# Joint maxima over two PSUM banks, one exponential for a global row, and K and Q transposed head by head, in a fused block-sparse attention and MLP kernel

## The chip, the cores and the metric

The kernel runs on one core of a Trainium2 chip. The time is the device time of one execution in microseconds (us), lower is better. The engines are named as in the profile: PE is TensorE (PEld its weight loads), DVE is VectorE, ACT is ScalarE, POOL is GpSimd, SP is SyncE, which here only issues DMAs. PSUM, into which TensorE writes, has eight banks of 512 float32 per partition; the kernel gives them out one by one.

## The reference, cut to what matters

Attention over 4 batches, 8 heads, 768 positions, head size 64, in blocks of 32 positions (24 blocks), with a mask: a query block sees its neighbours, the first and the last block, and three sampled blocks; the first and the last query block see everything. Its output, heads side by side, goes through a gated MLP (called MoE in the code) of 512 to 2048 to 512.

```python
scores = scale * np.matmul(q, k.transpose(0, 1, 3, 2))
scores = np.where(mask, scores, -1000000000.0)
scores = scores - np.max(scores, axis=-1, keepdims=True)
attn = np.exp(scores)
attn = attn / (np.sum(attn, axis=-1, keepdims=True) + 1e-09)
x = np.matmul(attn, v)            # then (B, H, S, D) -> (B * S, H * D)
h = x @ w_in
g = h * (1.0 / (1.0 + np.exp(-beta * h)))
out = g @ w_out
```

## The kernel before, in words

**Work and stages.** Each batch is prepared once: K, Q and V are loaded, K and Q are transposed by TensorE (`tr`, L460 to L468, four tasks for each of K and Q, one for two heads) and evicted into KT and QT (`ev`, L470). V is also written to a table in DRAM (VT, L490, L494). Then come 11 pairs of ordinary query blocks, 44 in all. For pair n: K blocks are gathered in SBUF on POOL and DVE (`kg`, `kn`), V blocks by DMAs from VT on SP's queue (`vg`, L582), `sc` (L595) makes the scores of all eight heads in two banks, `mx` (L621) the row maxima of each bank on DVE, `ex` (L627) the exponentials on ACT, two for each bank, `rc` and `nrm` (L635, L638) the normalisation, `tp` (L647) the transposes, `ptv` (L657) their eviction, `av` (L661) the product with V, and `xv` (L678) the copies into xT, the MLP's input. The two global query blocks of a batch go another way: `gs` (L700) fills four banks at once, with all 768 keys in two halves of 384 for each half of the heads, then `gm` (L717), `ge` (L724), `gr` (L732), `gn`, `gt`, `gptv`, and `gav` (L753), which multiplies with V for all four sets, and `gx` (L767), which copies into xT. In `gav` the 128 output rows are two heads and the 128 columns hold both row sets for both heads, of which a head needs half.

**The MLP** runs over eight groups of 8 or 16 blocks (L795). For a group, `h` (L814, product with w_in), `tanh` and `stt` (L823, L828) go sixteen times over slices of 128 hidden columns; then `y` (L842, product with w_out), `oe` and `od` (L854, L861).

**Loads of K, Q and V.** Batch 0 comes through SP in float32 and is cast by DVE into K16 and Q16 (L395), eight casts. Later batches come as float16 through POOL's queue (L442), two halves each, into two raw buffers: RAW[1] for K, RAW[0] for V and then for Q, so that a load of Q waits for V's copy out of that buffer. DVE then permutes them (`perm`, L447) from head-major into K16, Q16 or Vn, whose columns are all heads side by side, so that a transpose takes two heads at once: 128 columns by 128 rows, six of them to a task.

**Order.** Nothing is scheduled by the framework. Every piece of work is a `Task` with engine, modelled duration, dependences and priority; `Plan.run` simulates the machine and gives out engines and banks, always to the ready task of lowest priority number. Each engine then runs its tasks strictly in that order. A task that `opens` banks waits in the plan until as many are free (L104 to L107), any of the eight, and takes those that have been free longest (L119 to L121); the MLP may hold four while attention is left. Tasks that may run on one of several engines (`ev`, `kn`, `nrm`, `xv`, `gx`, `gn`) are given to the one that the model finds earliest. The waits at run time follow the data, not the plan, so where the model is off, an engine stands at a task whose input is late, and all behind it stand too.

Of the kernel before, what the change touches and what calls it, by code (L numbers as in the profile page):

```python
# [22 lines left out]
class Task:  # L23
    def __init__(self, name, eng, dur, emit, deps=(), prio=0.0, lat=0.0,
                 opens=(), closes=(), moe=False, dma=0.0, slack=0.0, hw=0, bulk=None):
        self.on = {eng: dur} if isinstance(eng, str) else dict(eng)
        self.name, self.eng, self.dur, self.emit = name, None, None, emit
        self.deps = [d for d in deps if d is not None]
        self.prio, self.lat = prio, lat
        self.opens, self.closes, self.moe, self.dma = opens, closes, moe, dma  # L30
        self.slack, self.hw, self.bulk = slack, hw, bulk
        self.kind = name.rstrip("0123456789.")
        self.end = None


class Plan:
# [9 lines left out]
    def add(self, *a, **k):  # L46
        t = Task(*a, **k)
        self.tasks.append(t)
        return t

    def run(self):
# [36 lines left out]
        while done < len(tasks):  # L88
            progress = False
            for e in engines:  # L90
# [3 lines left out]
                for t in waiting[e]:  # L94
                    if ready_at[t] > now + 1e-9:
                        continue
                    if len(t.on) > 1:
                        cost = {o: max(free[o], now) + d + BIAS.get((t.kind, o), 0.0)
                                for o, d in t.on.items()}
                        if cost[e] > min(cost.values()) + 1e-9:  # L100
                            continue
                    if t.bulk is not None and ring_at > now + t.bulk + 1e-9:
                        continue
                    if t.opens:  # L104
                        n_ok = sum(1 for f, _ in bank_free if f <= now + 1e-9)
                        if n_ok < len(t.opens):
                            continue  # L107
                        if t.moe and attention_left and held_moe + len(t.opens) > self.moe_banks:
                            continue
                    if best is None or t.prio < best.prio:  # L110
                        best = t
# [6 lines left out]
                if t.opens:  # L118
                    bank_free.sort()  # L119
                    for name in t.opens:  # L120
                        _, i = bank_free.pop(0)  # L121
                        self.bank[name] = i
                        if t.moe:
                            held_moe += 1
                            moe_owner.add(name)
                    if not t.moe:
                        attention_left -= 1
# [55 lines left out]
def kernel(  # L183
# [47 lines left out]
    K16 = sb("K16", [P, J, D_MODEL])  # L231
    Q16 = sb("Q16", [P, J, D_MODEL])
    RAW = [sb(f"RAW{i}", [P, H, J * D]) for i in range(2)]
# [14 lines left out]
    banks = [psum.tile([P, 512], FP32, name=f"bank{i}") for i in range(8)]  # L248
# [4 lines left out]
    bank16 = lambda name: banks[plan.bank[name]][:, :].bitcast(FP16)  # L253

# [131 lines left out]
    for i, (nm, t, dst) in enumerate((("K", k, K16), ("Q", q, Q16), ("V", v, None))):  # L386
        for f in range(2):
# [6 lines left out]
            for hp in range(2 * f, 2 * f + 2):  # L394
# [3 lines left out]
                        out=dst[:, :, hp * P:(hp + 1) * P].rearrange("p j (h d) -> p h j d", h=2),  # L398
                        in_=stage32(i, hp).rearrange("p h (j d) -> p h j d", j=J)),
# [31 lines left out]
    trK, trQ, evK, evQ, vperm, vtab, perm = {}, {}, {}, {}, {}, {}, {}  # L431
    later = {b: [] for b in range(B)}
    for b in range(B):
        pr = prep_prio(b)
        if b:
            vperm[b] = []
            for nm, t, raw, dst in (("V", v, RAW[0], Vn[b % 2]), ("K", k, RAW[1], K16), ("Q", q, RAW[0], Q16)):
                tr = {"K": trK, "Q": trQ}.get(nm)
                for f in range(2):
                    hs = slice(f * HH, (f + 1) * HH)  # L440
                    free = [vperm[b][f]] if nm == "Q" else [perm["QK"["VK".index(nm)], b - 1, f]] if b > 1 else []
# [5 lines left out]
                    tpm = add(f"perm{nm}{b}.{f}", "DVE", 0.55, lambda raw=raw, dst=dst, hs=hs: copy_on(  # L447
                        "DVE", dst[:, :, hs.start * D:hs.stop * D].rearrange("p j (h d) -> p h j d", h=HH),
                        raw[:, hs, :].rearrange("p h (j d) -> p h j d", j=J)),
                        deps=[tl] + ([tr[b - 1, hp] for hp in range(2 * f, 2 * f + 2)] if tr else []),  # L450
                        prio=pr - 5 * (nm == "V"))
                    if nm == "V":
                        vperm[b].append(tpm)
                    else:
                        perm[nm, b, f] = tpm
                        for hp in range(2 * f, 2 * f + 2):
                            ld[nm, b, hp] = tpm
        for nm, s16, dstT, tr, ev in (("K", K16, KT, trK, evK), ("Q", Q16, QT, trQ, evQ)):
            for hp in range(NHP):
                def emit_tr(nm=nm, s16=s16, b=b, hp=hp):  # L460
                    o = bank16((nm, b, hp))
                    for j in range(J):
                        nc.tensor.transpose(  # L463
                            out=o[:, j * P:(j + 1) * P],
                            in_=s16[:, j, hp * P:(hp + 1) * P],
                            identity=identity)
# [36 lines left out]
    for n, (b, p) in enumerate(order_pairs):  # L503
# [91 lines left out]
        def emit_sc(n=n, b=b, p=p, i0=i0, kgb=kgb):  # L595
# [11 lines left out]
            for g in range(2):  # L607
                for hp in range(NHP):
# [9 lines left out]
                    opens=(("S", n, 0), ("S", n, 1)))  # L618

        for u in range(2):  # L620
            mx[n, u] = add(f"mx{n}.{u}", "DVE", 0.6, lambda n=n, u=u, sb_=sb_: nc.vector.tensor_reduce(  # L621
                out=sb_[:, 0, 2 * u:2 * u + 2],
                in_=bank(("S", n, u))[:, :].rearrange("x (g c) -> x g c", g=2),
                axis=AX.X, op=ALU.max, negate=True),
                deps=[sc[n]] + ([nrm[n - NP]] if n >= NP else []), prio=pr)

# [6 lines left out]
            ex[n, u] = add(f"ex{n}.{u}", "ACT", 0.91, emit_ex, deps=[mx[n, u]] + (  # L633
# [60 lines left out]
    for b in range(B):  # L694
        for w, (blk, u) in enumerate((bl, u) for bl in (0, NB - 1) for u in range(2)):
# [15 lines left out]
            if u == 0:  # L711
                gs = add(f"gs{m}", "PE", 0.5, emit_gs, deps=[evK[b, hp] for hp in range(NHP)] +
                         [evQ[b, hp] for hp in range(NHP)], prio=pr, lat=0.2,
                         opens=tuple(("GS", m + uu, hf) for uu in range(2) for hf in range(2)))
                gsc_all.setdefault(b, []).append(gs)

            def emit_gm(m=m, s_=s_):  # L717
                for hf in range(2):
                    nc.vector.tensor_reduce(out=s_[:, hf:hf + 1], in_=bank(("GS", m, hf))[:, 0:S // 2],
                                            axis=AX.X, op=ALU.max, negate=True)  # L720
                nc.vector.tensor_reduce(out=s_[:, 2:3], in_=s_[:, 0:2], axis=AX.X, op=ALU.min)  # L721
            gm = add(f"gm{m}", "DVE", 1.15, emit_gm, deps=[gs] + ([gn[m - 2]] if m >= 2 else []), prio=pr)

            def emit_ge(m=m, s_=s_, pg=pg):  # L724
                for hf in range(2):
                    nc.scalar.activation(  # L726
                        out=pg[:, hf * (S // 2):(hf + 1) * (S // 2)], in_=bank(("GS", m, hf))[:, 0:S // 2],
                        func=AF.Exp, bias=s_[:, 2:3], scale=1.0, accum_out=s_[:, 3 + hf:4 + hf])
            ge = add(f"ge{m}", "ACT", 1.12, emit_ge, deps=[gm] + ([gt[m - 2]] if m >= 2 else []), prio=pr,
                     closes=(("GS", m, 0), ("GS", m, 1)))  # L730

            def emit_gr(s_=s_):  # L732
                nc.vector.tensor_reduce(out=s_[:, 5:6], in_=s_[:, 3:5], axis=AX.X, op=ALU.add)
                nc.vector.reciprocal(out=s_[:, 6:7], in_=s_[:, 5:6])
            gr = add(f"gr{m}", "DVE", 0.26, emit_gr, deps=[ge], prio=pr)
            gn[m] = add(f"gn{m}", {"POOL": 0.9, "DVE": 0.44}, None, lambda eng, s_=s_, pg=pg: (
                nc.vector if eng == "DVE" else nc.gpsimd).tensor_scalar(
                out=pg, in0=pg, scalar1=s_[:, 6:7], scalar2=1.0, op0=ALU.mult, op1=ALU.mult),
# [14 lines left out]
        def emit_gav(b=b):  # L753
            o = bank(("GO", b))
            first = True
            for hp in range(NHP):
                for j in range(J):
                    nc.tensor.matmul(
                        o[:, hp * P:(hp + 1) * P], lhsT=Vn[b % 2][:, j, hp * P:(hp + 1) * P],
                        rhs=PTG[:, j, :, hp * BLK:(hp + 1) * BLK],  # L760
                        start=first, stop=(j == J - 1), skip_group_check=True)
                    first = False
        gavt[b] = add(f"gav{b}", "PE", 1.4, emit_gav, deps=[gptv[gun - 4 + w] for w in range(4)] +
                      vperm[b], prio=pr, lat=0.2, opens=(("GO", b),))
        evs = []
        for u in range(2):
            def emit_gx(eng, u=u, b=b):  # L767
                src = bank(("GO", b))[u * D:(u + 1) * D, :].rearrange(
                    "x (h k v m) -> x h k v m", h=NHP, k=2, v=2)
                for kk, blk in enumerate((0, NB - 1)):  # L770
                    c0 = x_of(b * NB + blk)
                    dst = xT[u * D:(u + 1) * D, :, c0:c0 + BLK]
                    copy_on(eng, dst, src[:, :, kk, u, :])
            evs.append(add(f"gx{b}.{u}", {"DVE": 0.55, "ACT": 0.5}, None, emit_gx, deps=[gavt[b]], prio=pr,
                           closes=(("GO", b),)))
# [128 lines left out]
```

## Time and profile before

| | |
|---|---|
| median of 3 runs | 320.73 us (320.28 to 332.21) |
| profiled execution | 323.59 us, of which the span from first to last instruction is 321.8 us |
| mean granted TensorE clock | 0.929 |
| busy: PE, PEld | 280.7 us (87%), 177.3 us (55%) |
| busy: DVE, ACT, POOL | 246.7 us (77%), 216.8 us (67%), 187.5 us (58%) |
| `mx`, L621: 88 reductions, 128x512 | 57.5 us busy |
| `gm`, L719: 32 reductions, 128x384 | 16.1 us busy |
| `ge`, L726: 32 exponentials, 128x384, and their accumulator reads | 18.4 + 6.5 us busy |
| `perm` of K and of Q: 6 + 6 copies, 128x1536 | 5.4 + 3.7 us busy |
| `tr`, L463: 96 transposes of K, 96 of Q | 8.6 + 7.5 us busy |
| `gav`, L758: 96 matmuls | 6.0 us busy |

Busy times are sums of what an engine spent on a group of instructions; instructions that follow each other closely overlap by some tens of nanoseconds, so a group's busy time is a little under its count times its mean. Matmuls overlap much more: their own durations (219 ns for a 128-column one) say less than the distance from one to the next. In the chain of waits, each piece is put down to the work whose end released the next one.

### The profile page before, as it was taken

What the parts mean: (1) busy time and instruction counts of PE and PEld (TensorE: products, weight loads), DVE (VectorE), ACT (ScalarE), POOL (GpSimd) and SP (SyncE); (2) the same over time, 40 slices, a digit from 0 to 9 for tenths busy, and PEclk for the clock granted to TensorE, in tenths of its full rate; (3) what the DMA queues carried; (4) which work ended last, traced back from release to release, by engine and by line L of the source; (5) the groups of instructions that cost most, each with busy time, mean ns of one, the idle gap of its engine ahead of it and who ended that gap; (6) DMA issues with size and microseconds to landing.
All of it is one profiled execution on the core that took longest, in us unless ns stands there. A gap on an engine that the chain in (4) does not pass through costs nothing.

```text
span 321.8 us, 10665 instructions
## 1 busy us (share of the span) xinstructions
PE 280.7 (87%) x3525; PEld 177.3 (55%) x3525; DVE 246.7 (77%) x572; ACT 216.8 (67%) x644; POOL 187.5 (58%) x528
## 2 busy tenths in 40 slices
PE   0845578989979699988979999999999999999994
PEld 0612366956755486556635656555665555554671
DVE  2996579878869989999987667999979975771060
ACT  1676435864968489789687669977679864772361
POOL 2479956848778456798966654756948453200000
PEclk9975557999979989999979999999999999999999
DMA  7889995998697586323777973335232333100201
GB/s 255 332 172 208 229 227 105 187 252 177 132 204 145 164 212 114 107 80 94 125 146 168 226 170 93 88 84 153 94 118 69 91 110 100 33 3 33 98 2 66
DMA packets 42211, 43.97 MB, mean 137 GB/s; under 512 B 6440, under 2 KB 37672, under 8 KB 42156
## 3 DMA queue, kind: packets, MB, share of 16 engines
q1 hardware_dynamic: 27760, 25.71, 27.1%
q0 software_dynamic: 10784, 11.27, 23.4%
q10 hardware_dynamic: 3612, 6.30, 5.4%
q8 instruction: 28, 0.46, 0.6%
q14 instruction: 27, 0.22, 0.2%
HBM read 45.10 MB, written 9.44 MB: 169 GB/s over the span
## 4 chain that ended last, share of the span: by engine, by line
PE 60%; DMA 14%; DVE 12%; ACT 6%; issue 3%; SPq 3%; POOL 1%; POOLq 0%; ACTq 0%; DVEq 0%
PE bank L845 22%; PE bank L817 21%; DMA VG<-VT 6%; PE bank L668 4%; PE bank L653 4%; DMA RAW<-in_k_dram 3%; DMA VT<-Vn 3%; SPq L582 3%; DVE ST L621 2%; ACT PP L629 2%; PE bank L463 2%; DVE g L828 2%; PE bank L610 2%; PE bank L600 2%; DMA sbl<-in_sampled_blocks_dram 1%
## 5 line engine op out<-in xcount | busy, mean ns | idle before, releaser
L641 POOL TENSOR_SCALAR PP<-PP,ST 128x256 f16<-128x256 f16 x168 | 81.3, 501 | 47.9 <-DVE ST L635 42.4
L629 ACT ACTIVATE PP<-bank,ST 128x256 f16<-128x256 f32 x176 | 81.6, 478 | 30.1 <-DVE ST L621 21.5
L817 PE MATMUL bank<-xT,w_in_sb 128*128 128x256 f16 (+1 forms) x512 | 97.1, 338 | 3.9 <-ACT PP L629 1.1
L845 PE MATMUL bank<-w_out_sb,g 128*128 128x512 f16 x384 | 90.9, 380 | 0.0
L828 DVE SCALAR_TENSOR_TENSOR g<-t,bank 128x512 f16<-128x512 f16 (+1 forms) x128 | 66.6, 546 | 22.1 <-ACT t L823 21.3
L823 ACT ACTIVATE t<-bank,beta_sb 128x512 f16<-128x512 f32 (+1 forms) x128 | 69.9, 589 | 14.3 <-PE bank L817 11.6
L817 PEld LDWEIGHTS <-w_in_sb 128*128 128x128 f16 x512 | 55.3, 116 | 30.1 <-issue 8.6
L521 POOL COPY KG<-KT 128x64 f32 x264 | 54.6, 256 | 24.6 <-PE bank L610 17.8
L621 DVE TENSOR_REDUCE ST<-bank 128x2 f32<-128x512 f32 x88 | 57.5, 678 | 7.5 <-PE bank L610 7.4
L845 PEld LDWEIGHTS <-g 128*128 128x128 f16 x384 | 34.7, 98 | 38.6 <-issue 4.1
L668 PE MATMUL bank<-PT,VG 128*128 128x64 f16 x704 | 31.8, 199 | 7.9 <-DMA VG<-VT 5.9
L668 PEld LDWEIGHTS <-VG 128*128 128x128 f16 x704 | 28.3, 102 | 16.5 <-issue 9.6
L629 ACT ACTIVATION_READ_ACCUMULATOR PP<-bank,ST 128x1 f32 x176 | 36.8, 209 | 0.0
L653 PE MATMUL bank<-identity,PP 128*128 128x128 f16 x352 | 30.9, 233 | 6.6 <-ACT xT L257 2.4
L653 PEld LDWEIGHTS <-PP 128*128 128x128 f16 x352 | 24.6, 104 | 15.9 <-issue 4.1
L657 DVE COPY PT<-bank 128x1024 f16<-128x1024 f16 x44 | 30.1, 684 | 4.1 <-PE bank L653 3.3
L259 DVE CAST xT<-bank 64x256 f16<-64x256 f32 (+1 forms) x52 | 20.6, 402 | 12.3 <-PE bank L668 7.5
L263 ACT ACTIVATE osb<-bank 128x512 f32<-128x512 f32 x24 | 14.4, 601 | 20.7 <-PE bank L845 20.7
L257 ACT CAST xT<-bank 64x256 f16<-64x256 f32 (+1 forms) x52 | 17.4, 346 | 15.4 <-DVE xT L259 6.3
L610 PE MATMUL bank<-KG,QT 64*32 64x256 f16 x704 | 20.9, 293 | 1.4 <-POOL KG L521 1.0
L726 ACT ACTIVATE PG<-bank,SG 128x384 f16<-128x384 f32 x32 | 18.4, 583 | 4.9 <-DVE SG L721 4.1
L600 PE MATMUL bank<-maskr,ones 64*32 64x192 f16 (+1 forms) x352 | 14.9, 272 | 5.7 <-ACT PP L629 5.5
(79 smaller groups left out, 256.6 us busy)
## 6 DMA issues: line engine op xcount, KB each, us to landing
VG<-VT SPq DMA_DIRECT2D x268, 32.0 KB, 2.6
VG<-VT SPq DMA_DIRECT2D x40, 192.0 KB, 2.9
out_dram<-osb ACTq DMA_DIRECT2D x20, 256.0 KB, 2.2
RAW<-in_v_dram POOLq DMA_DIRECT2D x6, 384.0 KB, 5.1
RAW<-in_k_dram POOLq DMA_DIRECT2D x6, 384.0 KB, 5.6
VT<-Vn SPq DMA_DIRECT2D x3, 768.0 KB, 6.1
RAW<-in_q_dram POOLq DMA_DIRECT2D x6, 384.0 KB, 6.5
w_in_sb<-in_moe_w_in_dram POOLq DMA_DIRECT2D x8, 256.0 KB, 5.9
```

The source lines that it names most:

```text
L521: nc.gpsimd.tensor_copy(out=kg32[:, g, :, (2 + r) * W:(3 + r) * W], in_=kt32[:, :, bass.ds(vals[3 * g + r], W)])
L610: nc.tensor.matmul(bk[u][hp * BLK:(hp + 1) * BLK, g * 256:(g + 1) * 256], lhsT=QT[b % 2][u * D:(u + 1) * D, hp, (i0 + g) * BLK:(i0 + g + 1 ...
L621: mx[n, u] = add(f"mx{n}.{u}", "DVE", 0.6, lambda n=n, u=u, sb_=sb_: nc.vector.tensor_reduce(out=sb_[:, 0, 2 * u:2 * u + 2], in_=bank(("S" ...
L629: nc.scalar.activation(out=pb[:, u, g, :], in_=bank(("S", n, u))[:, g * 256:(g + 1) * 256], func=AF.Exp, bias=sb_[:, 0, 2 * u + g:2 * u + ...
L641: (nc.vector if eng == "DVE" else nc.gpsimd).tensor_scalar(out=pb[:, u, g, :], in0=pb[:, u, g, :], scalar1=sb_[:, 2, 2 * u + g:2 * u + g + ...
L653: nc.tensor.transpose(out=o[:, s * P:(s + 1) * P], in_=pb[:, u, g, c * P:(c + 1) * P], identity=identity)
L657: ptv[n] = add(f"ptv{n}", "DVE", 0.61, lambda n=n: nc.vector.tensor_copy(out=PT[n % NPT], in_=bank16(("T", n))), deps=[tp[n]] + ([av[n - N ...
L668: nc.tensor.matmul(o[:, (g * NHP + hp) * 64:(g * NHP + hp + 1) * 64], lhsT=vgb[:, g, c, hp * P:(hp + 1) * P], rhs=pt[:, g, c, :, hp * BLK: ...
L817: nc.tensor.matmul(o[:, 0:TW], lhsT=w_in_v[:, c, f // 4, f % 4, :], rhs=xT[:, c, c0:c0 + TW], start=(c == 0), stop=(c == NHP - 1))
L823: lambda G=G, f=f, TW=TW, tt=tt: nc.scalar.activation(out=tt[:, 0:TW], in_=bank(("H", G, f))[:, 0:TW], func=AF.Tanh, bias=0.0, scale=beta_ ...
L828: lambda G=G, f=f, TW=TW, tt=tt, gg=gg: nc.vector.scalar_tensor_tensor(out=gg[:, f, 0:TW], in0=tt[:, 0:TW], scalar=1.0, in1=bank(("H", G, ...
L845: nc.tensor.matmul(o[:, :], lhsT=gg[:, f, s * P:(s + 1) * P], rhs=w_out_sb[:, f, :], start=(f == 0), stop=(f == N_FFC - 1))
```

## The change

Six edits go together.

1. The eight banks are allocated as four tiles of two adjacent banks. `sc` and `gs` open banks in such twos (`twin=True`); a new `choose` finds whole pairs for them, and gives all other tasks banks whose neighbour is in use, where there is one.
2. `mx` is one task, one reduction over both banks (128x1024 into 4 columns) in place of two; both `ex` tasks depend on it.
3. `gm` is one reduction over 2 x 384, `ge` one exponential over 2 x 384 with one accumulator, `gr` one reciprocal.
4. K and Q have raw buffers of their own (RK, RQ; RV for V). The casts of batch 0 keep the head-major order, the permutations of K and Q are gone, and `tr` transposes each head by itself out of the raw buffer, 64 columns into 64 partitions, twelve to a task. A load of K or Q waits for the transposes of the batch before in place of permutations.
5. `gav` does each head by itself into its 64 partitions, with only the 64 columns that the head needs: 48 matmuls in place of 24.
6. The last block comes before the first in the global sets, so that both land side by side in xT, and `gx` is one copy in place of two tasks of two copies.

```diff
+    @staticmethod
+    def choose(t, bank_free, now):
+        at = {i: f for f, i in bank_free if f <= now + 1e-9}
+        whole = sorted((max(at[i], at[i + 1]), i) for i in at if i % 2 == 0 and i + 1 in at)
+        if t.twin:
+            if 2 * len(whole) < len(t.opens):
+                return None
+            return [i + h for _, i in whole[:len(t.opens) // 2] for h in range(2)]
+        if len(at) < len(t.opens):
+            return None
+        return sorted(at, key=lambda i: ((i ^ 1) in at, at[i], i))[:len(t.opens)]
...
-    banks = [psum.tile([P, 512], FP32, name=f"bank{i}") for i in range(8)]
+    twins = [psum.tile([P, 2, 512], FP32, name=f"bank{i}") for i in range(4)]
+    banks = [twins[i // 2][:, i % 2, :] for i in range(8)]
...
-                    free = [vperm[b][f]] if nm == "Q" else [perm["QK"["VK".index(nm)], b - 1, f]] if b > 1 else []
+                    if tr is None:
+                        free = [vperm[b - 1][f]] if b > 1 else []
+                    else:
+                        free = [tr[b - 1, hp] for hp in hps]
...
                     for j in range(J):
-                        nc.tensor.transpose(
-                            out=o[:, j * P:(j + 1) * P],
-                            in_=s16[:, j, hp * P:(hp + 1) * P],
-                            identity=identity)
+                        for u in range(2):
+                            nc.tensor.transpose(
+                                out=o[u * D:(u + 1) * D, j * P:(j + 1) * P],
+                                in_=s16[:, 2 * hp + u, j * D:(j + 1) * D],
+                                identity=identity, tile_position=(0, u * D))
...
+        mx[n] = add(f"mx{n}", "DVE", 1.2, lambda n=n, sb_=sb_: nc.vector.tensor_reduce(
+            out=sb_[:, 0, :], in_=twin(("S", n, 0))[:, :, :].rearrange("x u (g c) -> x (u g) c", g=2),
+            axis=AX.X, op=ALU.max, negate=True),
+            deps=[sc[n]] + ([nrm[n - NP]] if n >= NP else []), prio=pr)
...
+            gm = add(f"gm{m}", "DVE", 0.95, lambda m=m, s_=s_: nc.vector.tensor_reduce(
+                out=s_[:, 0:1], in_=twin(("GS", m, 0))[:, :, 0:S // 2], axis=AX.XY, op=ALU.max, negate=True),
+                deps=[gs] + ([gn[m - 2]] if m >= 2 else []), prio=pr)
+            ge = add(f"ge{m}", "ACT", 0.95, lambda m=m, s_=s_, pg=pg: nc.scalar.activation(
+                out=pg[:, :].rearrange("x (a c) -> x a c", a=2), in_=twin(("GS", m, 0))[:, :, 0:S // 2],
+                func=AF.Exp, bias=s_[:, 0:1], scale=1.0, accum_out=s_[:, 1:2]),
...
+                        nc.tensor.matmul(
+                            o[u * D:(u + 1) * D, hp * 2 * BLK:(hp + 1) * 2 * BLK],
+                            lhsT=Vn[b % 2][:, j, (2 * hp + u) * D:(2 * hp + u + 1) * D],
+                            rhs=PTG[:, j, u::2, hp * BLK:(hp + 1) * BLK],
+                            start=(hp + j == 0), stop=(j == J - 1), skip_group_check=True,
+                            tile_position=(0, u * D))
```

The modelled durations of `mx` (1.2, before 2 x 0.6), `gm` (0.95, before 1.15), `ge` (0.95, before 1.12), `gr` (0.1, before 0.26) and `gx` (0.42 on DVE or 0.38 on ACT, before 2 x 0.55 or 2 x 0.5) are new; those of `tr` (0.36) and `gav` (1.4) stay.

More of the change, by code (lines that the diff above doesn't have):

```diff
@@ L24, in __init__ @@
     def __init__(self, name, eng, dur, emit, deps=(), prio=0.0, lat=0.0,
-                 opens=(), closes=(), moe=False, dma=0.0, slack=0.0, hw=0, bulk=None):
+                 opens=(), closes=(), moe=False, dma=0.0, slack=0.0, hw=0, bulk=None, twin=False):
         self.on = {eng: dur} if isinstance(eng, str) else dict(eng)
@@ L30, in __init__ @@
         self.opens, self.closes, self.moe, self.dma = opens, closes, moe, dma
-        self.slack, self.hw, self.bulk = slack, hw, bulk
+        self.slack, self.hw, self.bulk, self.twin = slack, hw, bulk, twin
         self.kind = name.rstrip("0123456789.")
@@ L104, in run @@
                     if t.opens:
-                        n_ok = sum(1 for f, _ in bank_free if f <= now + 1e-9)
-                        if n_ok < len(t.opens):
+                        if self.choose(t, bank_free, now) is None:
                             continue
@@ L118, in run @@
                 if t.opens:
-                    bank_free.sort()
-                    for name in t.opens:
-                        _, i = bank_free.pop(0)
+                    picked = self.choose(t, bank_free, now)
+                    bank_free = [x for x in bank_free if x[1] not in picked]
+                    for name, i in zip(t.opens, picked):
                         self.bank[name] = i
@@ L230 @@
     QT = [sb(f"QT{i}", [P, NHP, S]) for i in range(2)]
-    K16 = sb("K16", [P, J, D_MODEL])
-    Q16 = sb("Q16", [P, J, D_MODEL])
-    RAW = [sb(f"RAW{i}", [P, H, J * D]) for i in range(2)]
+    RK, RQ, RV = (sb(f"R{x}", [P, H, J * D]) for x in "KQV")
     Vn = [sb(f"Vn{i}", [P, J, D_MODEL]) for i in range(2)]
@@ L253 @@
     bank16 = lambda name: banks[plan.bank[name]][:, :].bitcast(FP16)
+    twin = lambda name: twins[plan.bank[name] // 2]
     def copy_on(eng, out, in_):
@@ L385 @@
     v0ld = []
-    for i, (nm, t, dst) in enumerate((("K", k, K16), ("Q", q, Q16), ("V", v, None))):
+    for i, (nm, t, dst) in enumerate((("K", k, RK), ("Q", q, RQ), ("V", v, None))):
         for f in range(2):
@@ L397 @@
                     lambda i=i, dst=dst, hp=hp: nc.vector.tensor_copy(
-                        out=dst[:, :, hp * P:(hp + 1) * P].rearrange("p j (h d) -> p h j d", h=2),
-                        in_=stage32(i, hp).rearrange("p h (j d) -> p h j d", j=J)),
+                        out=dst[:, 2 * hp:2 * hp + 2, :], in_=stage32(i, hp)),
                     deps=[tl], prio=-72 + 4 * i + hp)
@@ L429, in prep_prio @@
         return -50 if b == 0 else 10 * (NPAIR * (b - 1) + 4)
-    trK, trQ, evK, evQ, vperm, vtab, perm = {}, {}, {}, {}, {}, {}, {}
+    trK, trQ, evK, evQ, vperm, vtab = {}, {}, {}, {}, {}, {}
     later = {b: [] for b in range(B)}
@@ L436 @@
             vperm[b] = []
-            for nm, t, raw, dst in (("V", v, RAW[0], Vn[b % 2]), ("K", k, RAW[1], K16), ("Q", q, RAW[0], Q16)):
+            for nm, t, raw in (("V", v, RV), ("K", k, RK), ("Q", q, RQ)):
                 tr = {"K": trK, "Q": trQ}.get(nm)
@@ L440 @@
                     hs = slice(f * HH, (f + 1) * HH)
-                    free = [vperm[b][f]] if nm == "Q" else [perm["QK"["VK".index(nm)], b - 1, f]] if b > 1 else []
+                    hps = range(2 * f, 2 * f + 2)
+                    if tr is None:
+                        free = [vperm[b - 1][f]] if b > 1 else []
+                    else:
+                        free = [tr[b - 1, hp] for hp in hps]
                     tl = add(f"ld{nm}{b}.{f}", "POOL", 0.9, lambda t=t, raw=raw, b=b, f=f, hs=hs:
@@ L446 @@
                     later[b].append(tl)
[L447 to L451, printed above, removed]
                     if nm == "V":
-                        vperm[b].append(tpm)
-                    else:
[L455 to L458, printed above, removed]
+                        vperm[b].append(add(f"permV{b}.{f}", "DVE", 0.55, lambda b=b, hs=hs: copy_on(
+                            "DVE", Vn[b % 2][:, :, hs.start * D:hs.stop * D].rearrange("p j (h d) -> p h j d", h=HH),
+                            RV[:, hs, :].rearrange("p h (j d) -> p h j d", j=J)), deps=[tl], prio=pr - 5))
+                    else:
+                        for hp in hps:
+                            ld[nm, b, hp] = tl
+        for nm, s16, dstT, tr, ev in (("K", RK, KT, trK, evK), ("Q", RQ, QT, trQ, evQ)):
             for hp in range(NHP):
@@ L617 @@
                     deps=[kg[n], kn[n], t_mask] + [evQ[b, hp] for hp in range(NHP)], prio=pr, lat=0.2,
-                    opens=(("S", n, 0), ("S", n, 1)))
-        for u in range(2):
[L621 to L625, printed above, removed]
+                    opens=(("S", n, 0), ("S", n, 1)), twin=True)
+        mx[n] = add(f"mx{n}", "DVE", 1.2, lambda n=n, sb_=sb_: nc.vector.tensor_reduce(
+            out=sb_[:, 0, :], in_=twin(("S", n, 0))[:, :, :].rearrange("x u (g c) -> x (u g) c", g=2),
+            axis=AX.X, op=ALU.max, negate=True),
+            deps=[sc[n]] + ([nrm[n - NP]] if n >= NP else []), prio=pr)
+        for u in range(2):
             def emit_ex(n=n, u=u, pb=pb, sb_=sb_):
@@ L632, in emit_ex @@
                         accum_out=sb_[:, 1, 2 * u + g:2 * u + g + 1])
-            ex[n, u] = add(f"ex{n}.{u}", "ACT", 0.91, emit_ex, deps=[mx[n, u]] + (
+            ex[n, u] = add(f"ex{n}.{u}", "ACT", 0.91, emit_ex, deps=[mx[n]] + (
                 [tp[n - NP]] if n >= NP else []), prio=pr, closes=(("S", n, u),))
@@ L694 @@
     for b in range(B):
-        for w, (blk, u) in enumerate((bl, u) for bl in (0, NB - 1) for u in range(2)):
+        for w, (blk, u) in enumerate((bl, u) for bl in (NB - 1, 0) for u in range(2)):
             pr = 10.0 * ((5, 11.5, 18, 31)[b] + 0.5 * w) + 5
@@ L713 @@
                          [evQ[b, hp] for hp in range(NHP)], prio=pr, lat=0.2,
-                         opens=tuple(("GS", m + uu, hf) for uu in range(2) for hf in range(2)))
+                         opens=tuple(("GS", m + uu, hf) for uu in range(2) for hf in range(2)), twin=True)
                 gsc_all.setdefault(b, []).append(gs)
[L717 to L735, printed above, removed]
+            gm = add(f"gm{m}", "DVE", 0.95, lambda m=m, s_=s_: nc.vector.tensor_reduce(
+                out=s_[:, 0:1], in_=twin(("GS", m, 0))[:, :, 0:S // 2], axis=AX.XY, op=ALU.max, negate=True),
+                deps=[gs] + ([gn[m - 2]] if m >= 2 else []), prio=pr)
@@ new lines @@
+            ge = add(f"ge{m}", "ACT", 0.95, lambda m=m, s_=s_, pg=pg: nc.scalar.activation(
+                out=pg[:, :].rearrange("x (a c) -> x a c", a=2), in_=twin(("GS", m, 0))[:, :, 0:S // 2],
+                func=AF.Exp, bias=s_[:, 0:1], scale=1.0, accum_out=s_[:, 1:2]),
+                deps=[gm] + ([gt[m - 2]] if m >= 2 else []), prio=pr,
+                closes=(("GS", m, 0), ("GS", m, 1)))
+            gr = add(f"gr{m}", "DVE", 0.1, lambda s_=s_: nc.vector.reciprocal(
+                out=s_[:, 2:3], in_=s_[:, 1:2]), deps=[ge], prio=pr)
@@ L736 @@
             gn[m] = add(f"gn{m}", {"POOL": 0.9, "DVE": 0.44}, None, lambda eng, s_=s_, pg=pg: (
                 nc.vector if eng == "DVE" else nc.gpsimd).tensor_scalar(
-                out=pg, in0=pg, scalar1=s_[:, 6:7], scalar2=1.0, op0=ALU.mult, op1=ALU.mult),
+                out=pg, in0=pg, scalar1=s_[:, 2:3], scalar2=1.0, op0=ALU.mult, op1=ALU.mult),
                 deps=[gr], prio=pr)
@@ L754, in emit_gav, with emit_gx @@
             o = bank(("GO", b))
-            first = True
             for hp in range(NHP):
                 for j in range(J):
[L758 to L762, printed above, removed]
+                    for u in range(2):
+                        nc.tensor.matmul(
[4 more added lines that the diff above has]
+                            tile_position=(0, u * D))
         gavt[b] = add(f"gav{b}", "PE", 1.4, emit_gav, deps=[gptv[gun - 4 + w] for w in range(4)] +
                       vperm[b], prio=pr, lat=0.2, opens=(("GO", b),))
[L765 to L775, printed above, removed]
+        def emit_gx(eng, b=b):
+            c0 = x_of(b * NB + NB - 1)
+            copy_on(eng, xT[:, :, c0:c0 + 2 * BLK],
+                    bank(("GO", b))[:, 0:2 * NHP * BLK].rearrange("x (h m) -> x h m", h=NHP))
+        evs = [add(f"gx{b}", {"DVE": 0.42, "ACT": 0.38}, None, emit_gx, deps=[gavt[b]], prio=pr,
+                   closes=(("GO", b),))]
         for blk in (0, NB - 1):
```

## The prediction

> **What bounds the kernel now.** I read the slices first, then busy time by stretch, then what TensorE waited for, then the chain of waits. Slices (8 us each):
>
> ```profile
> PE   0845578989979699988979999999999999999994
> DVE  2996579878869989999987667999979975771060
> PEclk9975557999979989999979999999999999999999
> DMA  7889995998697586323777973335232333100201
> ```
>
> TensorE is thin for seven slices, while the DMA engines stand at 7 to 9, and nearly full from slice 20. Busy time in four stretches (after the stretch its length, then each engine's busy us, the clock, the DMA share, GB/s):
>
> ```profile
> core 0: us, PE busy (x) PEld busy (x) DVE busy (x) ACT busy (x) POOL busy (x), PEclk, DMA share, GB/s
> 0.00:55.00 55.00, 30.51 (x438) 20.59 (x439) 40.43 (x115) 28.25 (x93) 36.80 (x109) 0.71 0.87 219
> 55.00:100.00 45.00, 40.78 (x575) 30.18 (x573) 36.93 (x90) 32.57 (x101) 32.55 (x91) 0.94 0.93 186
> 100.00:163.00 63.00, 55.63 (x826) 38.07 (x824) 59.40 (x141) 49.26 (x158) 47.29 (x124) 0.97 0.57 135
> 163.00:318.00 155.00, 153.83 (x1692) 88.44 (x1692) 109.91 (x230) 106.76 (x296) 70.90 (x206) 0.99 0.36 95
> ```
>
> Before 55 us weights and V gathers bound it (DMA 0.87; TensorE idle 24.5 us). From 163 us TensorE is busy 153.8 of 155: relief of another engine buys nothing there, and added TensorE work costs its full length. Between 100 and 163 us VectorE has 59.4 of 63 and TensorE idles 7.4. What TensorE waited for there (total, times, longest):
>
> ```profile
> PE bank L653 <- ACT xT L257: 2.4, 2, 1.7
> PE bank L668 <- DVE PT L657: 1.9, 1, 1.9
> PE bank L817 <- ACT xT L257: 0.8, 1, 0.8
> PE bank L817 <- ACT PP L629: 0.7, 2, 0.4
> PE bank L817 <- ACT PG L726: 0.7, 1, 0.7
> PE bank L817 <- DVE g L828: 0.4, 1, 0.4
> PE bank L817 <- ACT QT L263: 0.3, 1, 0.3
> ```
>
> The seven lines sum to 7.2 us. The chain there (start, length):
>
> ```profile
> 144.74 1.02 DVE SG L719 x2
> 145.78 0.15 DVE SG L721
> ...
> 152.65 1.29 DVE ST L621 x2
> 153.94 0.47 DVE PTG L747
> ...
> 157.45 2.41 DVE KG L259 x3
> ...
> 162.23 0.61 DVE PT L657
> ```
>
> It runs through VectorE almost piece after piece: maxima, evictions, copies. This is the stretch in which the change can pay.
>
> **The change, part by part.**
>
> *Joint pair maximum.* 88 reductions of 512 (median 681 ns) become 44 of 1024. From 384 elements (547) to 512 the slope is 134/128 = 1.047 ns an element, so 681 + 512 × 1.047 = 1.22 us; two now take 1.29, saving 0.07 × 44 = 3 us of VectorE. No row reads two banks at once: bounds 1.07 (slope alone) and 1.36 (two separate ones, a loss of 0.07 each); I take 1.22, the row's own slope. But the first exponential now waits for both halves, 1.22 − 0.68 = 0.54 us more. Behind it on ScalarE stand tanh and evictions; ScalarE's idle 13.7 of the 63 us hides it, and if that cover is gone it costs 0.54 a pair (a rival below).
>
> *Global rows.* Two reductions and a combine take 144.74 to 145.93, 1.19 us; one over 768 is 547 + 384 × 1.047 = 0.95, saving 0.24 × 16. Two exponentials and accumulator reads pace at 1.13 (110.56 to 111.69); one of 768 by the slope (583 − 478)/128 = 0.82 ns is 583 + 315 = 0.90, plus 0.09 for the read: 0.14 × 16 saved on ScalarE. The sum of two halves (16 × 0.14) goes.
>
> *K and Q permutations.* Twelve VectorE copies go (5.4 + 3.7 = 9.1 us busy). The first batch's eight casts keep their size and stay at 0.55. VectorE stood behind loads in these copies (2.5 and 1.8 us); that wait now falls on TensorE, with w_out matmuls queued behind the transpose and tanh and evictions waiting for those. TensorE already waited 1.0 there (71.2 to 72.2). Bounds: 1.0 gained to 4.3 − 1.0 = 3.3 lost; I take 0, since the same hop goes and the same load remains.
>
> In 100 to 163 us VectorE loses: permutations 2.5 + 1.2, pair maxima 9 × 0.07, global maxima 8 × 0.24, sums 1.15: 7.4 us of 59.4.
>
> *Transposes by head.* 192 of 128 columns become 384 into 64 partitions. Eighteen now take 1.00 us, 55.6 ns each. If the two column halves stream together, twelve take what six did (0.33 us); if one after the other, 0.67. Bounds 0 and +0.33 for each of 32 tasks. I take 0: the score matmuls, on eight positions, run sixteen of 256 columns from 171.04 to 171.38, 21 ns each, against 863/8 = 108 ns that half of a 512-column matmul takes. Row halves alone could give two at once; here five run.
>
> *Global value matmuls.* 24 take 1.34 us. 48 of half the columns take 0.67 if halves run together and 1.34 if not: 0 to 0.67 saved, four times; I take half, 1.35 in all. Change of array shape: before scores TensorE left 0.1 us (w_in starts at 169.99, needs 0.86, scores start at 170.95). Fourteen runs of transposes after batch 0 and four value blocks: 18 × 0.11 = 2.0. TensorE's sum: +0.65. Loads dearer than this: a rival.
>
> The Trainium skill ("TensorEngine Tiling (Array Packing)", Restrictions and Gotchas) says that column tiling excludes Fast Weight Load, a rule against this change; "TensorE: Matmul & The Clock Gate" (LDWEIGHTS) gives columns/1.2 ns, by estimate 53 ns for 64. Loaded one after another, the twelve would take 0.64 us and the sum would be 24 × 0.31 = 7.4 us worse. The trace has no 128x64 form; its 32-column loads, tiled too, start sixteen within 0.19 us.
>
> *Output copies.* Sixteen copies of 64x128 (2.1 + 1.5 us) become four of 128x256 (0.37 to 0.42): 2 us off both engines, mostly behind TensorE. Last block first: nothing, both blocks need the same K and Q.
>
> *Loads.* The same 18 DMAs on POOL's queue, 0.8 us each. Q no longer waits for V's copy; before, the Q loads left at 67.95, well after V's copies at 59.1 and 62.6, so no earlier start: 0. K and Q of batch 1 now wait for transposes done at 14.6, loads leave from 60.4: 0. If loads did move up, gathers would share the engines (DMA 0.93): up to the 1.5 us that one gather already cost TensorE. SP's queue has the same DMAs in the same order.
>
> *Banks in twos.* Scores need a whole pair, global scores two pairs. I take 0 since single users fill broken pairs first; the upper end is a rival.
>
> **Sum.** Of the 7.2 us, 1.75 + 0.65 stand behind an output DMA (ScalarE waits 2.8 for it at 107) and stay: 4.8 can go. The clock fell at the 1.9 us stall at 163 (four matmuls took 1.71 instead of 0.86, sixteen value matmuls 0.82 instead of 0.47): 1.2. So −4.8 − 1.2 + 0.65 = −5.35. The profiled execution took 323.6 (span 321.8), 2.9 above the median 320.7; 318.2 from it, and from the median **315.4**.
>
> **Rivals.**
>
> *D, everything clears.* Relief also lets the plan bridge the gather and output waits: all TensorE idle from 55 to 163 us, 4.2 + 7.4 = 11.6, and both clock drops, 1.2 and 1.27 (twelve w_in matmuls at 111.8 took 2.57, not 1.30), less 0.65: 307.3. For it: VectorE gains 7.4 us of air. Against: DMA stays at 0.93 up to 100 us.
>
> *E, the relief becomes another wait.* The later first exponential costs its 0.54 for each of the stretch's nine pairs, 4.8: 320.2. For it: ScalarE waited for this maximum 17 times, 21.5 us. Against: in this stretch only 2.5 us of them.
>
> *B, column halves don't overlap (slower).* Each half-width instruction paces like a full one, 55.6 ns: 24 transposing tasks after batch 0 × 0.33 = 8.0, value blocks 4 × (2.67 − 1.34) = 5.3, shape changes 2.0, less the 6.0 of relief: 330.0. The page's missing fast load would work this way. Against: the 21 ns above.
>
> *C, the pairing starves scores (slower).* A score block that finds two single banks must wait. In the first 55 us TensorE waited for a bank of an exponential 5 times, 5.5 us: 1.1 each. From 55 to 163 us there are 16 score and 4 global openings; five blocked ones eat the gain, eleven make it 2% slower; twelve give 320.7 − 5.35 + 13.2 = 328.6. For it: MoE may hold four banks. Against: other TensorE work fills many such waits.
>
> **How the numbers follow.** About 2% (6.4 us) is what a measurement of this kernel can tell from no change: faster means under 314.3, slower over 327.1. The forecast has 0.46, with 311 to 319 as its own range; 0.18 of it lies under 314.3. D 0.15, E 0.10, B 0.11, C 0.18 (0.14 of it slower, 0.04 within). Faster 0.18 + 0.15 = 0.33; slower 0.11 + 0.14 = 0.25; the same 0.42. The range runs from D to C's 328; outside lie some of B and C and a little of D, under 0.2.
>
> **What would show it.** Right: one 1024-element reduction near 1.22 us and one 768 exponential near 0.90; no copies out of RAW but V's; twelve transposes still near 0.33 us; VectorE near 52 us in the stretch before TensorE saturates; that saturation some 5 us earlier. Wrong: transposes near 0.67 (B); score matmuls waiting for exponentials (C); ScalarE waiting longer for maxima (E); transposes waiting for loads. A plan that orders the work quite differently would make the whole sum wrong, since it goes by the old order's stalls.

## The result and the profile after

The changed kernel takes 381.74 us (median of 4 runs) against 326.37 before: ratio 1.191, interval 1.182 to 1.201. The forecast was 315.4, the range 307 to 328. The profiled execution has a span of 380.1 us. The kernel before was timed anew for each comparison below, and some executions, of either kernel, take 1 to 4% longer than the rest (332 us in two of four here); ratios leave these out, so they can differ a little from the ratio of the two medians.

The slices of the changed kernel, now 9.5 us each:

```profile
PE   1745478885987688887788997997888987878894
DVE  3884466763696677866875457774468642651060
PEclk9999999999699999989999999998999999999998
DMA  7699979964658651583187721322231231000201
```

TensorE does not fill: mostly 7s and 8s stand where the kernel before had a row of 9s. VectorE is emptier too (60% of the span busy, before 77%), so no engine took over as the bound. Busy time in the same stretches of the changed kernel, and one more:

```profile
55.00:100.00 45.00, 35.82 (x541) 26.03 (x539) 28.33 (x64) 26.74 (x77) 21.91 (x66) 0.94 0.78 161
100.00:163.00 63.00, 49.32 (x864) 33.68 (x862) 48.34 (x97) 44.68 (x146) 42.24 (x115) 0.99 0.57 126
163.00:318.00 155.00, 133.92 (x1708) 74.72 (x1709) 98.67 (x175) 96.40 (x271) 82.80 (x241) 0.98 0.39 97
318.00:380.00 62.00, 47.58 (x276) 25.75 (x275) 18.80 (x37) 25.07 (x51) 2.32 (x6) 0.99 0.09 30
```

From 163 to 318 us TensorE idles 21 us of 155, before 1.2. VectorE, ScalarE and GpSimd have no more work than before over the span (227.0, 216.1 and 184.0 us busy, before 246.7, 216.8 and 187.5) and are idle more, which is what waits on each other look like. TensorE's busy time did rise, 280.7 to 294.4 us; but it is 295.4 in the run tile_only below, which has the matmuls of the kernel before, and 279.1 in the changed kernel without the loss (after_one_tile), so that rise belongs to the waits and not to the work. Each new instruction, though, costs what the prediction gave it (last figure before the second bar: busy; after it: mean ns):

```profile
L632 DVE TENSOR_REDUCE ST<-bank 128x4 f32<-128x1024 f32 x44 | 53.3, 1213 | 4.3 <-PE bank L622 4.3
L727 DVE TENSOR_REDUCE SG<-bank 128x1 f32<-128x768 f32 x16 | 14.7, 946 | 0.1
L730 ACT ACTIVATE PG<-bank,SG 128x768 f16<-128x768 f32 x16 | 14.5, 907 | 8.0 <-DVE SG L727 7.0 <-DVE SG L735 0.5 <-ACT osb L275 0.4
L760 PE MATMUL bank<-PTG,Vn 128*64 128x64 f16 x192 | 3.8, 197 | 0.0
```

What is new is whom the w_out matmuls wait for. They need `g` and a bank of their own. In the kernel before their only idle time in the trace was (`issue` is time in which the engine waited for nothing that the profile shows)

```profile
its engine sat idle before it (us, times) until:
  issue: 4.1, 18
```

and in the changed kernel it was

```profile
its engine sat idle before it (us, times) until:
  issue: 20.5, 42
  ACT osb L275: 3.9, 7
  DVE PT L667: 2.3, 4
  DVE g L826: 2.2, 3
  ACT xT L269: 1.7, 3
  DVE PTG L748: 0.8, 1
```

PT (an eviction of transposes), xT and PTG are nothing that a w_out matmul reads. What such an eviction shares with it is the PSUM it comes from: either the same bank, handed on to the matmul, or the other bank of its tile. The runs below tell which.

### The profile page after: what moved, and what is told of

It is laid out like the page before. It is cut to its first block, busy times and chain, and to the rows that moved or that the text cites. A ratio compares the mean times of both kernels' runs of the same rounds, so it can differ in the third digit from the quotient of the medians.

```text
span 380.1 us, 11048 instructions
## 1 busy us (share of the span) xinstructions
PE 294.4 (77%) x3813; PEld 180.0 (47%) x3813; DVE 227.0 (60%) x457; ACT 216.1 (57%) x611; POOL 184.0 (48%) x528
## 4 chain that ended last, share of the span: by engine, by line
PE 43%; DVE 18%; ACT 16%; DMA 12%; issue 5%; SPq 3%; ACTq 1%; POOL 1%; POOLq 0%; DVEq 0%
PE bank L843 19%; PE bank L815 10%; DMA VG<-VT 7%; DVE g L826 6%; ACT t L821 6%; PE bank L678 5%; ACT PP L639 4%; PE bank L663 3%; DMA VT<-Vn 3%; DVE PT L667 3%; SPq L594 3%; PE bank L475 3%; ACT osb L275 2%; ACT xT L269 2%; DVE xT L271 1%
## 5 line engine op out<-in xcount | busy, mean ns | idle before, releaser
L815 PE MATMUL bank<-xT,w_in_sb 128*128 128x256 f16 (+1 forms) x512 | 99.2, 335 | 19.9 <-DVE g L826 6.7
L843 PE MATMUL bank<-w_out_sb,g 128*128 128x512 f16 x384 | 93.6, 383 | 11.8 <-ACT osb L275 3.9
L821 ACT ACTIVATE t<-bank,beta_sb 128x512 f16<-128x512 f32 (+1 forms) x128 | 69.7, 580 | 41.1 <-PE bank L815 16.7
L533 POOL COPY KG<-KT 128x64 f32 x264 | 51.8, 245 | 33.5 <-PE bank L622 24.5
L632 DVE TENSOR_REDUCE ST<-bank 128x4 f32<-128x1024 f32 x44 | 53.3, 1213 | 4.3 <-PE bank L622 4.3
L678 PE MATMUL bank<-PT,VG 128*128 128x64 f16 x704 | 32.9, 199 | 14.6 <-DMA VG<-VT 5.3
L269 ACT CAST xT<-bank 64x256 f16<-64x256 f32 (+1 forms) x52 | 19.0, 365 | 38.6 <-PE bank L678 11.9
L271 DVE CAST xT<-bank 64x256 f16<-64x256 f32 (+1 forms) x40 | 16.9, 421 | 35.3 <-ACT xT L269 26.5
L663 PEld LDWEIGHTS <-PP 128*128 128x128 f16 x352 | 25.7, 106 | 21.5 <-POOL PP L651 7.6
L275 ACT ACTIVATE osb<-bank 128x512 f32<-128x512 f32 x24 | 14.3, 597 | 31.8 <-PE bank L843 21.5
L738 POOL TENSOR_SCALAR PG<-PG,SG 128x768 f16<-128x768 f16 x13 | 12.1, 934 | 17.6 <-DVE SG L735 9.1
L730 ACT ACTIVATE PG<-bank,SG 128x768 f16<-128x768 f32 x16 | 14.5, 907 | 8.0 <-DVE SG L727 7.0
```

What stands on the lines that cost most here:

```text
L269: nc.scalar.copy(out=out, in_=in_)
L533: nc.gpsimd.tensor_copy(out=kg32[:, g, :, (2 + r) * W:(3 + r) * W], in_=kt32[:, :, bass.ds(vals[3 * g + r], W)])
L632: mx[n] = add(f"mx{n}", "DVE", 1.2, lambda n=n, sb_=sb_: nc.vector.tensor_reduce(out=sb_[:, 0, :], in_=twin(("S", n, 0))[:, :, :].rearrang ...
L663: nc.tensor.transpose(out=o[:, s * P:(s + 1) * P], in_=pb[:, u, g, c * P:(c + 1) * P], identity=identity)
L678: nc.tensor.matmul(o[:, (g * NHP + hp) * 64:(g * NHP + hp + 1) * 64], lhsT=vgb[:, g, c, hp * P:(hp + 1) * P], rhs=pt[:, g, c, :, hp * BLK: ...
L815: nc.tensor.matmul(o[:, 0:TW], lhsT=w_in_v[:, c, f // 4, f % 4, :], rhs=xT[:, c, c0:c0 + TW], start=(c == 0), stop=(c == NHP - 1))
```

## The experiments

**Theory T:** the run-time waits follow tiles, so that a user of one bank of a two-bank tile waits for users of the other. **Rivals:** P, the pairing in the plan (C of the prediction); M, the transposes, loads or joint instructions.

### The tile alone

```diff
-    banks = [psum.tile([P, 512], FP32, name=f"bank{i}") for i in range(8)]
+    twins = [psum.tile([P, 2, 512], FP32, name=f"bank{i}") for i in range(4)]
+    banks = [twins[i // 2][:, i % 2, :] for i in range(8)]
```

> The kernel before, with one edit: its eight banks are halves of four two-bank tiles; plan, order on every engine, instructions and bank choice stay as before. Theory T (the run-time waits follow the tile, so an instruction on one bank also waits for the users of the other bank of its tile): most of the 60 us come back with this edit alone, 360 to 385 us, and VectorE and ScalarE wait for each other on evictions as in the changed kernel. Theory P (the pairing in the plan starves score blocks) and theory M (transposes, loads or joint maxima): about the time of the kernel before, 318 to 333 us.

385.38 us against 322.72: 1.199 (1.187 to 1.210). This edit alone, in the kernel before, makes the whole loss. One such wait, TensorE's timeline and then VectorE's (start, length, work, and idle time before it with its releaser):

```profile
204.46 1.89 PE L846 MATMUL bank<-w_out_sb,g 128*128 128x512 f16 x8 [0.92 <-DVE ST L622]
206.64 1.02 PE L846 MATMUL bank<-w_out_sb,g 128*128 128x512 f16 x4 [0.29 <-ACT PP L630]
```

```profile
203.74 0.66 DVE L622 TENSOR_REDUCE ST<-bank 128x2 f32<-128x512 f32 x1
```

A w_out product already under way (the first eight of its sixteen matmuls had run from 201.64) stops for 0.92 us, and goes on 0.06 us after a maximum of scores ends at 204.40. Nothing in the data joins the two.

### Everything but the tile

Eight one-bank tiles in the changed kernel; `mx`, `gm` and `ge` then issue one instruction for each bank.

```diff
-    twins = [psum.tile([P, 2, 512], FP32, name=f"bank{i}") for i in range(4)]
-    banks = [twins[i // 2][:, i % 2, :] for i in range(8)]
+    banks = [psum.tile([P, 512], FP32, name=f"bank{i}") for i in range(8)]
```

> The changed kernel with eight tiles of one bank each; the pairing in the plan, the head-by-head transposes, the loads and the value matmuls stay. As no instruction can then span two banks, the maxima are two reductions again and a global row has two exponentials, inside the same tasks. Theory T: 312 to 325 us, as the kernel before or a little under. Theory P: 370 to 385 us. Theory M for transposes or loads: over 350 us; for the joint instructions: about 320 us, which the run above tells from T.

326.96 us: 1.014 (0.995 to 1.033). The loss of 60 us is gone, though the time lies 2 us above T's range. Then without the pairing:

```diff
-        if t.twin:
+        if False:
...
-        return sorted(at, key=lambda i: ((i ^ 1) in at, at[i], i))[:len(t.opens)]
+        return sorted(at, key=lambda i: (at[i], i))[:len(t.opens)]
```

> The run above with the old choice of banks too (any free ones, those free longest): what is left of the change is transposes by head, own raw buffers, half-width value matmuls, and the first exponential behind both maxima. Theory T: 312 to 325 us, within 5 us of the run above. Theory P: far below the run above, near 320 us against 370. Theory M for transposes or loads: over 350 us.

328.98 us: 1.022 (1.009 to 1.035), 4 us above T's range; the parts of the change that this run still has are tried one by one further down. And the pairing alone, `choose` and `twin=True` in the kernel before:

> The kernel before, with the pairing in the plan alone (scores open whole pairs, other tasks fill broken pairs first); eight tiles of one bank each, all else as before. Theory T: 318 to 330 us. Theory P (rival C of the prediction): 328 us or more, most of the way to 380 if it is the whole cause.

324.78 us: 1.013 (1.000 to 1.025). P falls as the cause.

### Half the dose, and score banks of their own

```diff
+    banks = [psum.tile([P, 512], FP32, name=f"bank{i}") for i in range(4)]
+    twins = [psum.tile([P, 2, 512], FP32, name=f"twin{i}") for i in range(2)]
+    banks += [twins[i // 2][:, i % 2, :] for i in range(4)]
```

> The kernel before with banks 4 to 7 alone as halves of two two-bank tiles, banks 0 to 3 as before; plan and orders unchanged. Theory T (users of the two banks of a tile wait for each other): a part of the 63 us that four such tiles cost, about half, so 340 to 365 us. Rival (some other effect of the tile edit, such as where the banks lie): either no loss, 319 to 328 us, or all of it, 380 us and more.

359.23 us against 325.48: 1.101 (1.085 to 1.116), half of the 20%. Next the changed kernel with two two-bank tiles for scores alone:

```diff
-        at = {i: f for f, i in bank_free if f <= now + 1e-9}
+        at = {i: f for f, i in bank_free if f <= now + 1e-9 and (i < 4) == t.twin}
...
-    plan = Plan(8, 4)
+    plan = Plan(8, 3)
```

> The changed kernel with two two-bank tiles that only score blocks and global scores use, four banks of one tile each for all else, and at most three of these for the MLP. All joint instructions stay. Theory T: most of the loss goes, 322 to 345 us, since the two halves of such a tile now belong to one score block; what is left is the fixed split of the banks, which the next run has too. If joint instructions or two-bank reads cost time by themselves: 360 us or more.

335.61 us: 1.039 (1.031 to 1.046). The control, the same split over one-bank tiles:

> Control for the run above: the same fixed split of banks, with eight tiles of one bank and separate maxima and exponentials. Theory T: within 6 us of the run above, above it by what the joint instructions save or under it by what is left of waits in the score tiles. If joint instructions cost time by themselves: 20 us or more under the run above.

333.17 us: 1.032 (1.024 to 1.040). So a two-bank tile does little harm (2.4 us between these medians, and the two intervals overlap) where both banks belong to one block of scores. The control has most of the 3 to 4% too: it is the price of the fixed split, with three banks for the MLP, on top of the 1.014 of the same kernel without a split.

### One tile of all eight banks: theory T falls as stated

```diff
+    whole = psum.tile([P, 8, 512], FP32, name="whole")
+    banks = [whole[:, i, :] for i in range(8)]
```

> The kernel before with all eight banks as parts of one tile; plan and orders unchanged. Theory T: waits between users of all banks, so far more than the 63 us of four two-bank tiles: 450 us or more. If only neighbouring banks matter, or waits are only for the instruction just before: 380 to 400 us.

The two runs took 323.49 and 332.89 us, those of the kernel before 322.34 to 334.31, where T said 450 or more. Banks of one tile do not always wait for each other. The new form, T2: only a tile larger than a bank and smaller than all of PSUM makes them wait. Two more kernels tried it. The kernel before with two tiles of four banks:

```diff
+    parts = [psum.tile([P, 4, 512], FP32, name=f"part{i}") for i in range(2)]
+    banks = [parts[i // 4][:, i % 4, :] for i in range(8)]
```

> The kernel before with its eight banks as parts of two four-bank tiles; plan and orders unchanged. T2: slow, at least as slow as two-bank tiles, 385 us or more, since a bank has three others to wait for. If larger tiles are treated better (the one tile of eight lost nothing): 322 to 350 us.

559.46 us: 1.735 (1.716 to 1.754). What TensorE waited for there:

```profile
PE part L818 <- DVE g L829: 21.1, 19, 2.5
PE part L818 <- ACT PP L630: 14.6, 9, 2.9
PE part L846 <- ACT PP L630: 12.0, 7, 2.9
```

Both MLP products now wait for the exponentials of attention, 26.6 us; in the kernel before it was 1.1. And the changed kernel in one tile:

```diff
+    whole = psum.tile([P, 8, 512], FP32, name="whole")
-    twins = [psum.tile([P, 2, 512], FP32, name=f"bank{i}") for i in range(4)]
+    twins = [whole[:, 2 * i:2 * i + 2, :] for i in range(4)]
```

> The changed kernel with one edit: its four two-bank tiles become parts of one tile of all eight banks; all joint instructions, the pairing and the rest stay as they are. Theory T2 (only a tile that is larger than a bank and smaller than the whole PSUM makes users of one of its banks wait for those of another): the whole loss goes, 318 to 330 us, and the joint instructions are seen at their worth for the first time. Theory T3 (the loss needs a two-bank tile and the joint instructions or the pairing add their own): 345 us or more.

321.59 us against 323.89: 0.995 (0.988 to 1.002). Every instruction of the change is in it, the joint reads of two banks too, and the 60 us are gone. Its stretches:

```profile
55.00:100.00 45.00, 41.91 (x662) 30.13 (x661) 35.62 (x83) 34.28 (x106) 27.04 (x73) 0.98 0.81 171
100.00:163.00 63.00, 56.37 (x964) 37.67 (x962) 55.61 (x111) 50.67 (x153) 47.69 (x133) 0.97 0.64 147
163.00:318.00 155.00, 150.79 (x1752) 85.99 (x1750) 97.76 (x175) 103.51 (x284) 71.38 (x211) 1.00 0.35 95
```

TensorE is nearly full again from 163 us on (150.8 of 155, before 153.8). Why a tile of all eight banks keeps its banks apart and one of two or four does not stays open: the runs show the effect, not the rule that the recording layer follows.

### The smaller parts

Edit 4 alone in the kernel before:

```diff
+    RK, RQ, RV = (sb(f"R{x}", [P, H, J * D]) for x in "KQV")
...
+                                in_=s16[:, 2 * hp + u, j * D:(j + 1) * D],
+                                identity=identity, tile_position=(0, u * D))
```

> The kernel before with edit 4 alone: own raw buffers, no permutations of K and Q, transposes by head. By the prediction's terms (permutations off VectorE in the stretch from 100 to 163 us, transposes at no cost, the load wait now on TensorE): 316 to 323 us. If the load wait on TensorE or an unlucky order of loads in the first 100 us is what makes the two runs without the tile 1 to 2% slower: 324 to 330 us.

322.77 us against 325.48: 0.992 (0.986 to 0.998). With edits 5 and 6 on top (`gav` and `gx` as in the change):

> The kernel before with edits 4, 5 and 6 (transposes by head, half-width value matmuls, last block first with one copy), without pairing, two-bank tiles or joint instructions. If the 1 to 2% lost without the tile come from the maxima taken as one task, this is a little under the kernel before, 0.98 to 1.00 of it, as the transposes alone are. If they come from edits 5 and 6 or from how these shift the plan: 1.01 to 1.03.

323.54 against 326.27: 0.993 (0.988 to 0.998). Rival E, in the kernel before:

```diff
-            ex[n, u] = add(f"ex{n}.{u}", "ACT", 0.91, emit_ex, deps=[mx[n, u]] + (
+            ex[n, u] = add(f"ex{n}.{u}", "ACT", 0.91, emit_ex, deps=[mx[n]] + (
```

> The kernel before with both maxima of a pair as one task of the plan (two instructions still, one bank each), on which both exponential tasks depend. Rival E of the prediction (the later first exponential eats the relief): 1.01 to 1.03 of the kernel before. If the plan's dependence does not matter: 0.99 to 1.01.

328.97: 1.010 (1.005 to 1.016). Last, the changed kernel in one tile without edit 2 (two `mx` tasks as before, no `twin=True` for `sc`):

> The run above with one tile, less edit 2: each bank of a pair has its own maximum and its exponentials depend on that alone, and score blocks take any two banks; the joint maximum and exponential of global rows stay, as do edits 4 to 6. If the maximum as one task costs 1%, as measured, and the pairing some of the rest: 316 to 323 us, the fastest of all. If the joint maximum is worth what the prediction gave it: slower than the changed kernel in one tile.

320.80 against 323.89: 0.995 (0.989 to 1.001), no different from the run with edit 2.

## Why the prediction was wrong, point by point

**The step that failed** is "Banks in twos … I take 0 since single users fill broken pairs first". It took the new tiles for a matter of the plan alone, which bank a task may open, and asked what the plan would do. But the waits at run time come from the tile in which an instruction is recorded. The term that stood at 0 measured 0.199 of 322.7, 64 us, and no rival had it: C, nearest in words, was about score blocks waiting in the plan, and alone (pairs_only) measured 1.3% (0.0 to 2.5%), 4 us, where it was priced at 13. The text even had the piece needed, that each engine stands at a task whose input is late and all behind it with it; so one false wait on TensorE holds the MLP, attention and, through them, both evicting engines.

**What the prediction's sum was worth** shows in one tile: 0.995 of the kernel before, 1.5 us gained, with an interval from 3.8 gained to 0.8 lost, where −5.35 was forecast. This takes it that the one tile costs nothing by itself, which its two runs in the kernel before tell no closer than some per cent.

- *Joint instructions*: 1.213, 0.946 and 0.907 us against 1.22, 0.95 and 0.90. Right.
- *Transposes by head, and the change of array shape*: both right. In the lines below twelve take 173.64 − 173.18 = 0.46 us to the next instruction, thirty-six 176.18 − 175.06 = 1.12. The difference is 0.66 for twenty-four, 28 ns each, so twelve cost the 0.33 that six full ones did; the other 0.13 comes once in a run, where the next work has another shape, and was priced at 0.11.
- *Global value matmuls*: 167.86 − 166.98 = 0.88 us where 24 full ones took 1.34, so 0.46 is saved each time, the change of shape included. With the thirteen runs of transposes after batch 0 in this trace (13 × 0.13 = 1.7 lost, 4 × 0.46 = 1.8 saved) TensorE's own sum is about nothing, where it was +0.65. These lines are of the changed kernel in one tile:

```profile
166.98 0.95 PE L761 MATMUL whole<-PTG,Vn 128*64 128x64 f16 x48
167.86 0.28 PE L613 MATMUL whole<-maskr,ones 64*32 64x192 f16 x8
173.18 0.53 PE L476 MATMUL whole<-identity,RK 128*64 128x128 f16 x12
173.64 1.04 PE L844 MATMUL whole<-w_out_sb,g 128*128 128x512 f16 x4
175.06 1.20 PE L476 MATMUL whole<-identity,RK 128*64 128x128 f16 x36
176.18 1.04 PE L844 MATMUL whole<-w_out_sb,g 128*128 128x512 f16 x4
181.10 0.53 PE L476 MATMUL whole<-identity,RQ 128*64 128x128 f16 x12 [0.83 <-DMA RQ<-in_q_dram]
```

- *Rival B*: excluded by the same lines, 28 ns where it needed 55.6. Nor do twelve take the 0.64 us that was estimated for loads one after another. The Trainium skill's rule ("TensorEngine Tiling (Array Packing)", Restrictions and Gotchas) that column tiling excludes Fast Weight Load does not show in this pace; whether the loads were fast ones, no run here tells.
- *The load wait on TensorE*: it moved there as said. The last line shows 0.83 us of it; with 0.6 for K in the stretch before, it is 1.4 after the first 100 us. Before, TensorE's wait for a permutation was 1.0, at 71.2.
- *VectorE's relief*: 246.7 us became 224.4 over the span. In the stretch from 100 to 163 us only 59.4 became 55.6, not 52, since the new order put other work in: eleven pair maxima in place of nine, and twelve 512-column `g` instructions in place of eight.
- *Which stalls go* (4.8 us, and 1.2 of clock): mis-sized. In one tile TensorE still idles 63 − 56.4 = 6.6 us in the stretch, before 7.4, and over the whole span 40.4, before 41.1. The stretch's granted clock is 0.97 in both. What TensorE waited for there:

```profile
PE whole L679 <- DVE PT L668: 1.8, 3, 1.0
PE whole L816 <- DVE xT L272: 1.8, 1, 1.8
PE whole L664 <- ACT PG L731: 1.5, 1, 1.5
```

  The lines that were to go were replaced by others of the same size. I had counted stalls of the old order as if they had been made by the engines that released them; a new plan makes its own. That the plan's order, with the modelled durations, makes most of them is argued, not shown.
- *Rival E*: the edit that makes the first exponential wait for both maxima costs something, but not by the wait that E named. It measured 1.0%, 3.3 us, where E was priced at 4.8. Yet ScalarE stood 7 times, 11.8 us, for these maxima in that run, and 17 times, 21.5 us, in the kernel before; in the stretch that E counted, both had one such wait of 1.1 us:

```profile
ACT PP L631 <- DVE ST L622: 11.8, 7, 3.8
```

  By which path the edit costs its 1.0% stays open; that a task of 1.2 us changes what the plan does with everything else is possible, and not shown. In one tile the kernel takes the same with and without edit 2 (0.995 both).

By its ratio no version here beats the kernel before by more than 1%: edit 4 alone (0.992) and edits 4 to 6 (0.993) are the only ones whose interval lies under 1.

## What to carry to other kernels

When a change regroups buffers, ask what the waits are kept on. A larger tile can join users whose data never meet, and in an engine that runs in a fixed order each such wait holds all that follows; so price it as a term of its own, and test it by making the regrouping alone in the old kernel. When all engines get emptier at once and instruction times are as forecast, look for releasers that the data cannot explain. And count a stall as removable only if what ends it gets faster in the new order too.

## What the runs showed of the hardware

A reduction by VectorE over two neighbouring PSUM banks keeps the pace of one bank: 1213 ns for 1024 elements, against 1.22 from the slope of 384 and 512. ScalarE does too, 907 ns for 768, against 0.90 from the slope of 256 and 384. Transposes into 64 partitions, two column halves in turn, go at 28 ns each, so two take as long as a full-width one, 55.6; a run of them costs 0.13 us more before work of another shape.
